# Attention into a gated feed-forward: the hidden units dealt four to a row, beta in sixteen pieces, and an earlier request for four units of q and k

## The chip, the core and the metric

The kernel runs on one core of a Trainium2 chip, written in Bass, with every instruction placed by hand or by the kernel's own planner. The core has TensorE (PE, with its weight loads shown as PEld), VectorE (DVE), ScalarE (ACT), GpSimd (POOL) and SyncE (SP). Transfers are issued by SP, ACT and POOL; those that change the type from float32 to bfloat16 on the way are all issued by POOL. The metric is the device time of one execution in microseconds (us). The kernel before took a median of 228.8 us in three runs (228.58 to 229.22).

## The reference

Attention over 4 batches, 8 heads, 768 positions and 64 dimensions. A query sees its own and the 127 positions before it, and the first four positions (the sinks). The result, 3072 tokens of 512 values, goes through a feed-forward with 2048 hidden units:

```
scores = scale * q @ k^T; keep = (pos < 4) or (0 <= i - j < 128)
a = softmax(scores where keep);  x = (a @ v) laid out as (3072, 512)
h = x @ w_in                      # (3072, 2048)
g = h * sigmoid(beta * h)         # beta has one value per hidden unit
out = g @ w_out                   # (3072, 512), float32
```

The kernel computes sigmoid by tanh: g' = h * (tanh(beta/2 * h) + 1), and halves the output.

## The kernel before

**Attention** is cut into 32 units: a unit is one pair of heads and one half (384 positions) of one batch. For units 0 to 11, q and k come in as float32 through SP (`load_qk`, line 522), are cast to bfloat16 (`cast`, line 621: k always on POOL; q on DVE for units 0 to 3, on POOL after that), transposed on PE (`transpose_first`, `transpose_in`, lines 652 and 634) and copied out of PSUM by DVE or ACT. Scores go through ACT's exponential, a mask on DVE, the product with v (`attend`, line 770), a division (`normalise`, lines 779 and 781) and a transpose into `xT`. Units 12 to 31 come in already as bfloat16 (`land_qk`, `land_v`, lines 552 and 561, issued by POOL) and are transposed by DMA.

**The feed-forward** takes the tokens in 8 tiles of 384 (T) and the hidden units in 16 blocks of 128 (m). `hidden_matmul` (line 814) makes a block's 128x384 from four matmuls, whose stationary operand is a 128x128 piece of `w_in16`. `tanh` on ACT (line 822) scales by a column of `beta_half`, `gate` on DVE (line 835) writes `g`, and `project` (line 843) multiplies with `w_out16`, 512 columns wide. In the first tile the blocks use four PSUM banks, two of which (`acc0`, `acc1`) are later the accumulators of `project`; block 12 and block 15 are their last users. While the second half of the first batch is attended (units 4 to 7), only products of the first tile can run beside it: the hidden blocks of the second tile need the outputs of units 4 to 7.

**The weights** come in through POOL: `w_in` in four chunks of four blocks (512 KB as bfloat16, 1 MB as read; line 578), `w_out` in eight chunks of two blocks (256 KB, 512 KB as read; line 583). A row of `w_out` is 2 KB; block m of it is rows 128m to 128m+127, so partition p of a chunk gets two rows that lie 256 KB apart, as two runs of 2 KB. Beta comes as 16 rows of 128 into 16 partitions (line 864, issued by ACT), and one transpose on PE (line 883) turns it into 128x16.

**The order** of each engine's instructions is fixed when the kernel is built. A planner (`Prog.order`, `round`, `landings`) takes the instructions in the order in which the program names them, with durations and a model of the transfers written in the code, and gives each engine, whenever it is free, the instruction that could start first; between equals, the one named earlier. On the chip an engine then works through its list and waits where a semaphore says so. So a change of one request or one duration may move any instruction of any engine. `after=` holds a transfer back until something has landed: the loads of units 4 to 7 wait for the second chunk of `w_in`, those of units 8 to 11 for `w_out` chunks 4, 6, 8 and 10 (named by their first block), and the v loads of the second batch for `w_out` 6, 8:

```
load_qk(y, x, [("w_in", 0, 4)])          # units 4 to 7, on SP
load_qk(n, x, [("w_out", 2 * n - 12)])   # units 8 to 11, on SP
load_v(2, c, [("w_out", 2 * c + 6)])     # on POOL
```

Between 12 and 35 us POOL's list is: the `w_in` chunks between casts, `k_sink` filled and the masks made (lines 444, 440, 492), two small loads of sink values, three loads of v for units 4 to 7 (line 542), the first `w_out` chunk, and then the casts of units 4 to 7 between the other seven `w_out` chunks.

Of the kernel before, what the change touches and what calls it, by code (L numbers as in the profile page):

```python
# [5 lines left out]
F32 = mybir.dt.float32  # L6
AF = mybir.ActivationFunctionType
ALU = mybir.AluOpType

B, H, S, D = 4, 8, 768, 64  # L10
NSINK, WINDOW = 4, 128
DM, DF, NOUT = 512, 2048, 512
NTOK = B * S
NPAIR = B * (H // 2)
SCALE = 1.0 / (D ** 0.5)
# [3 lines left out]
TT = 384  # L19
NT = NTOK // TT  # L20
NU = 4 * NT
NM = DF // 128
# [33 lines left out]
AGENDA = {}  # L56
for n in range(4, 8):
    for step, at in (("in", n - 4), ("sink", 16), ("a", 16), ("b", 16), ("av", 17), ("out", 18)):
        AGENDA.setdefault(at if step == "in" else at + 1 * (n - 4), []).append((n, step))
for n in range(8, NU):  # L60
    for at, step in STEPS.items():
        AGENDA.setdefault(FIRST[n] + at, []).append((n, step))
# [294 lines left out]
def bass_streamingllm_window__then__act_swish_beta_kernel(  # L357
# [21 lines left out]
    def sb(name, shape, dtype):  # L379
        ctx.append(nc.sbuf_tensor(name, list(shape), dtype))  # L380
        return ctx[-1].__enter__()
# [5 lines left out]
    xT = sb("xT", (128, 4, NTOK), BF16)  # L387
    w_in16 = sb("w_in16", (128, 4, DF), BF16)
    w_out16 = sb("w_out16", (128, NM, NOUT), BF16)
    beta_stage = sb("beta_stage", (16, 128), F32)  # L390
    beta_half = sb("beta_half", (128, NM), F32)
    ones = sb("ones", (128, 128), BF16)
    zeros = sb("zeros", (128, 384), BF16)
# [2 lines left out]
    ident32 = sb("ident32", (32, 32), F32)  # L396
# [30 lines left out]
    def pe(n):  # L427
        return {"busy": 2.5 + n / 2.4, "lag": 260.0}
# [4 lines left out]
    def dve(t):  # L433
        return {"busy": t, "lag": 140.0}
# [82 lines left out]
    def load_qk(n, x, after=(), queue="sp"):  # L517
        _, _, half, pb = place(n)
        name = "qk"[x]
        s = rows_of((q, k)[x], n, 1, half, 3)  # L520
        d = stage[name][pb][:, :, 3 * half:3 * half + 3, :].rearrange("p h c d -> p h (c d)")
        op(queue, lambda e: e.dma_start(d, s), w=[(name + "_stage", pb, half)], after=after,  # L522
           dma=f"{name}{pb}_{half}", seq="loads " + queue, **transfer(2 * TT * D * 4, 290 if n not in (1, 2) or x else 170, 520.0))
# [47 lines left out]
           w=[("qkT", pb, half)], dma=f"t{pb}{half}", busy=1300.0, lag=1300.0)  # L571

    w_in_src = moe_w_in.rearrange("(c p) f -> p c f", p=128)
    w_out_src = moe_w_out.rearrange("(m p) n -> p m n", p=128)

    def load_w_in(m, ms, after=()):
        here = slice(m * 128, (m + ms) * 128)
# [2 lines left out]
           dma=f"wi{m}", late=0.0 if m else 800.0, **transfer(DM * ms * 128 * 4, 385, 740.0, 3.0))  # L580

    def load_w_out(m, ms, after=()):
        op("gp", lambda e: e.dma_start(w_out16[:, m:m + ms, :], w_out_src[:, m:m + ms, :]), after=after,
           w=[("w_out", mm) for mm in range(m, m + ms)],
           dma=f"wo{m}", **transfer(ms * 128 * NOUT * 4, 416, 740.0, 3.0))

# [28 lines left out]
    def cast(n):  # L615
        _, _, half, pb = place(n)
        z = n % NQK
        here = slice(3 * half, 3 * half + 3)
        for x, name in enumerate("qk"):
            eng = "dve" if n < 4 and x == 0 else "gp"  # L620
            op(eng, lambda e, x=x, name=name, eng=eng: (e.copy if eng == "act" else e.tensor_copy)(  # L621
                qk16[z][:, x, :, :, :], stage[name][pb][:, :, here, :].rearrange("p h c d -> p c h d")),
               r=[(name + "_stage", pb, half)], w=[(name + "16", z)],
               **(dve(300.0) if eng == "dve" else {"busy": 460.0, "lag": 100.0}))
# [186 lines left out]
    def hidden_matmul(i, c):  # L811
        T, m = i // NM, i % NM
        bank, name = hidden_bank(i)
        op("pe", lambda e: e.matmul(  # L814
            bank, w_in16[:, c, m * 128:(m + 1) * 128], xT[:, c, T * TT:(T + 1) * TT],
            start=(c == 0), stop=(c == 3)),
           r=[("w_in", c, m), ("xT", T, c)], w=[name], **pe(TT))

# [22 lines left out]
    def project(T, t, m, bank, name, eng="act", cols=slice(0, NOUT), queue="sp"):  # L841
# [19 lines left out]


    constants()
    op("act", lambda e: e.dma_start(beta_stage[:, :], moe_beta.rearrange("(m p) -> m p", p=128)),
       w=["beta_stage"], dma="beta", busy=500.0, lag=100.0)
    for n in range(4):
        for x in range(2):
# [1 line left out]
    for c in range(6):  # L869
        load_v32(c // 3, c % 3)  # L870
    op("act", lambda e: e.activation(scratch[:, :], ones32[:, 0:1], AF.Exp, bias=0.0, scale=1.0),
       r=["ones32"], w=["scratch"], busy=1500.0)
    cast(0)
    cast(1)
    cast_v(0)
# [4 lines left out]

    select(ident32[:, :], ones32[:, :], [[1, 32]], ALU.is_equal, 0.0, 0, -1, ["ones32"], ["ident32"])
    transpose_first(0)
    op("pe", lambda e: nc.tensor.transpose(acc[1][:, 0:16], beta_stage[:, :], ident32[0:16, 0:16]),
       r=["beta_stage", "ident32"], w=["acc1"], **pe(64))
    op("dve", lambda e: e.tensor_scalar(beta_half[:, :], acc[1][:, 0:16], 0.5, None, ALU.mult),
       x=["acc1"], w=["beta"], **dve(100.0))

    def first_scores(n):
# [12 lines left out]
    for n in range(4):  # L901
        if n < 2:
            transpose_first(n + 2)
        if n < 3:
            first_scores(n + 1)
        if n == 2:
            for y in range(4, 8):
                for x in range(2):
                    load_qk(y, x, [("w_in", 0, 4)])
            fill("gp", k_sink[:, :, :], 0.0, ["k_sink"], busy=1800.0, after=[("v", 3, 0, 0)])  # L910
            masks([("v", 3, 0, 0)])
            load_sinks(0, [("v", 3, 0, 0)])
            for c in range(3):
                load_v(1, c, [("v", 3, 0, 0)])
            load_w_out(0, 2, [("v", 3, 0, 0)])
        bank = (acc[1], "acc1") if n < 3 else (h_ps[:, 0, :], "h0")
        attend(n, *bank)
        normalise(n, *bank)
# [122 lines left out]
```

## Time and profile before

| | |
|---|---|
| time of the profiled execution | 228.59 us |
| its span | 226.9 us |
| median of three runs | 228.8 us |
| PE busy | 220.0 us of the span |
| ACT, DVE, POOL busy | 141.3, 132.6, 125.7 us |
| hidden matmul, four of a block back to back | 0.65 us |
| granted TensorE clock | full throughout |
| read from HBM | 27.34 MB |

The span is what lies between the first and last instruction of the program; 1.7 us lie around it. A busy PE in these rows includes the tail of each matmul, which overlaps the next, so a PE that shows 2.00 of 2.00 us has no hole, and one that shows less has at least that hole. Sizes in the DMA rows of queue q0 (POOL's) are the bytes written, in bfloat16; twice as many were read. Queue q1 is SP's.

### The profile page before, as it was taken

The numbers are of one execution on the slowest core, as the hardware profiler recorded it, in microseconds if no ns is written. First come the engines' busy times: TensorE is split into PE (matmuls) and PEld (weight loads), VectorE is DVE, ScalarE is ACT, GpSimd is POOL, SyncE is SP. The second block draws the span as 40 slices with busy tenths as digits, with TensorE's granted clock in tenths as the row PEclk, the third lists the DMA queues.
The fourth block names the chain that finished last, engine by engine and source line by source line (L and its number), as shares of the span: only waits on it lengthen the run. The fifth ranks groups of instructions, "written<-read, shape, count | busy, mean of one in ns | idle before, by whom it ended". The sixth has DMA issues, their size and how long they took to land.

```text
span 226.9 us, 4463 instructions
## 1 busy us (share of the span) xinstructions
PE 220.0 (97%) x1761; PEld 122.1 (54%) x1761; DVE 132.6 (58%) x264; ACT 141.3 (62%) x224; POOL 125.7 (55%) x191
## 2 busy tenths in 40 slices
PE   7999989999999999999999999999999999999995
PEld 4665545555555555555555555555555555555454
DVE  5466777488975776566565656555656564443200
ACT  1877796197586877566657766666656755555311
POOL 4689992899994979695939396876300000000000
PEclk9999999999999999999999999999999999999999
DMA  6999999999998999999999999998921012110122
GB/s 172 251 172 179 276 194 205 257 228 139 118 138 124 124 117 151 120 167 144 116 113 135 99 138 147 96 165 119 94 80 53 20 57 64 49 46 0 58 83 92
DMA packets 96901, 28.92 MB, mean 127 GB/s; under 512 B 83424, under 2 KB 93936, under 8 KB 96880
## 3 DMA queue, kind: packets, MB, share of 16 engines
q0 software_dynamic: 59232, 10.92, 65.7%
q1 hardware_dynamic: 34304, 16.79, 34.3%
q10 hardware_dynamic: 3344, 0.93, 1.9%
q8 instruction: 14, 0.23, 0.5%
q14 instruction: 7, 0.06, 0.1%
HBM read 27.34 MB, written 6.29 MB: 148 GB/s over the span
## 4 chain that ended last, share of the span: by engine, by line
PE 73%; DMA 15%; POOL 8%; issue 2%; SPq 1%; ACT 0%; POOLq 0%; ACTq 0%
PE acc L843 32%; PE h_ps L814 29%; DMA k_stage<-in_k_dram 8%; DMA w_out<-in_moe_w_out_dram 4%; PE s_ps L727 4%; PE s_ps L770 4%; POOL qk L621 3%; DMA w_in<-in_moe_w_in_dram 2%; POOL land L552 2%; PE h_ps L843 2%; POOL v_aug L561 1%; PE s_ps L759 1%; PE s_ps L670 1%; SPq L522 1%; POOL v_aug L532 0%
## 5 line engine op out<-in xcount | busy, mean ns | idle before, releaser
L822 ACT ACTIVATE th<-h_ps,beta_half 128x384 f32<-128x384 f32 x120 | 69.4, 581 | 59.7 <-PE h_ps L814 59.1
L843 PE MATMUL acc<-w_out,g 128*128 128x512 bf16 x368 | 99.7, 380 | 0.0
L814 PE MATMUL h_ps<-xT,w_in 128*128 128x384 bf16 x480 | 96.2, 326 | 0.0
L835 DVE SCALAR_TENSOR_TENSOR g<-th,h_ps 128x384 bf16<-128x384 f32 x120 | 65.6, 550 | 44.8 <-ACT th L822 44.0
L814 PEld LDWEIGHTS h_ps<-xT,w_in 128*128 128x128 bf16 x480 | 45.6, 98 | 39.8 <-issue 0.8
L843 PEld LDWEIGHTS acc<-w_out,g 128*128 128x128 bf16 x368 | 32.8, 98 | 28.8 <-issue 3.6
L552 POOL DMA_DIRECT2D land<-in_q_dram x40 | 30.2, 760 | 24.0 <-DVE rden L779 24.0
L552 POOL DMA_DIRECT2D land<-in_k_dram x40 | 30.3, 761 | 0.0
L561 POOL DMA_DIRECT2D v_aug<-in_v_dram x40 | 30.2, 760 | 0.0
L735 ACT ACTIVATE E<-s_ps 128x1536 bf16<-128x1536 f32 x20 | 28.8, 1442 | 0.0
L741 DVE TENSOR_TENSOR E<-E,mask 128x1536 bf16<-128x1536 bf16 x20 | 19.2, 958 | 16.4 <-ACT E L735 16.4
L851 ACT ACTIVATE out_sb<-acc 128x512 f32<-128x512 f32 x23 | 13.7, 596 | 7.6 <-PE acc L843 7.4
L770 PEld LDWEIGHTS s_ps<-v_aug,E 128*128 128x128 bf16 x336 | 15.2, 97 | 3.2 <-issue 1.2
L770 PE MATMUL s_ps<-v_aug,E 128*128 128x65 bf16 x336 | 16.8, 193 | 0.0
L707 ACT ACTIVATE E<-s_ps 128x768 bf16<-128x768 f32 x17 | 13.7, 811 | 4.3 <-PE s_ps L700 4.2
L781 DVE TENSOR_TENSOR o_norm<-s_ps,rden 128x384 bf16<-128x384 f32 x28 | 15.6, 556 | 0.8
L714 DVE TENSOR_TENSOR E<-E,mask 128x768 bf16<-128x768 bf16 x16 | 9.0, 572 | 2.0 <-ACT E L707 1.3
L727 PE MATMUL s_ps<-qkT 64*128 64x256 bf16 (+2 forms) x144 | 10.1, 254 | 0.0
L759 PE MATMUL s_ps<-v_sink,E_sink 128*128 128x130 bf16 x48 | 9.3, 219 | 0.0
L621 POOL CAST qk<-k_stage 128x384 bf16<-128x384 f32 x12 | 6.5, 544 | 4.7 <-DMA k_stage<-in_k_dram 4.4
L673 ACT ACTIVATE E_sink<-s_ps 128x384 bf16<-128x384 f32 x16 | 7.8, 490 | 1.5 <-PE s_ps L670 1.5
L727 PEld LDWEIGHTS s_ps<-qkT 64*128 64x128 bf16 x144 | 4.9, 94 | 7.1 <-issue 5.8
(75 smaller groups left out, 155.2 us busy)
## 6 DMA issues: line engine op xcount, KB each, us to landing
out_dram<-out_sb SPq DMA_DIRECT2D x23, 256.0 KB, 2.7
q_stage<-in_q_dram SPq DMA_DIRECT2D x12, 192.0 KB, 7.4
k_stage<-in_k_dram SPq DMA_DIRECT2D x12, 192.0 KB, 7.9
w_in<-in_moe_w_in_dram POOLq DMA_DIRECT2D x4, 512.0 KB, 6.8
w_out<-in_moe_w_out_dram POOLq DMA_DIRECT2D x8, 256.0 KB, 9.6
land<-in_q_dram POOLq DMA_DIRECT2D x40, 48.0 KB, 3.7
land<-in_k_dram POOLq DMA_DIRECT2D x40, 48.0 KB, 4.0
v_aug<-in_v_dram POOLq DMA_DIRECT2D x40, 48.0 KB, 3.4
```

The costliest lines, as they stand in the source:

```text
L552: op("gp", lambda e, d=d, s=s: e.dma_start(d, s), w=[("land", pb, half, x, hh)], after=after, dma=f"l{pb}{half}{x}{hh}", **transfer(TT * D ...
L561: op("gp", lambda e, d=d, s=s: e.dma_start(d, s), w=[("v", pb, 3 * half + c, hh) for c in range(3)], after=after, dma=f"lv{pb}{half}{hh}", ...
L707: op("act", lambda e: e.activation(both, src[:, :, 0:TT], AF.Exp, bias=0.0, scale=SCALE), x=list(names), w=[("E", n % NE, c)], **act(768))
L727: op("pe", lambda e, at=at, w=w, kb=kb, qb=qb, nq=nq, hh=hh, rows=rows, bank=bank: e.matmul(s_ps[:, 2 * hh + bank, at:at + w], keys_of(pb, ...
L735: op("act", lambda e: e.activation(E[z][:, :, :], src, AF.Exp, bias=0.0, scale=SCALE), x=list(S_NAMES), w=[("E", z, 0), ("E", z, 1)], **ac ...
L741: op("dve", lambda e: e.tensor_tensor(E[z][:, :, :], E[z][:, :, :], m.unsqueeze(1).to_broadcast([128, 2, 768]), ALU.mult), r=[("E", z, 0), ...
L770: last=(x == len(kbs) - 1): e.matmul(av_ps[:, at + hh * D1:at + hh * D1 + D1], E[z][:, hh, col:col + 128], v_aug[:, pb, hh, kb, 0:D1], sta ...
L781: op("dve", lambda e: e.tensor_tensor(o_norm[o][:, :, :, :].rearrange("p m h d -> p (m h) d"), src[:, :, 0:D], rden[z][:, :].unsqueeze(2). ...
L814: op("pe", lambda e: e.matmul(bank, w_in16[:, c, m * 128:(m + 1) * 128], xT[:, c, T * TT:(T + 1) * TT], start=(c == 0), stop=(c == 3)), r= ...
L822: op("act", lambda e: e.activation(th[i % 3][:, :], bank, AF.Tanh, bias=0.0, scale=beta_half[:, m:m + 1]), x=[name], r=["beta"], w=[("th", ...
L835: op("dve", lambda e: e.scalar_tensor_tensor(g[T % 2][:, m, :], th[i % 3][:, :], 1.0, bank, ALU.add, ALU.mult), r=[("th", i % 3)], x=[name ...
L843: op("pe", lambda e: e.matmul(bank[:, 0:width], g[T % 2][:, m, t * 128:(t + 1) * 128], w_out16[:, m, cols], start=(m == 0), stop=(m == NM ...
```

## The change

Four things change together.

1. The hidden units are dealt to blocks in another way. Within each group of 512 units, block 4g+j now holds units 512g + 4p + j (p from 0 to 127) instead of 128 neighbours. Partition p of a `w_out` chunk then reads two rows that are neighbours, one run of 4 KB. The columns of `w_in16` that a hidden matmul loads as its stationary operand are now every fourth one: a step of 8 bytes in place of 2. How `w_in` is loaded does not change.
2. Beta follows the same deal. It is loaded as sixteen pieces of 128 values into four partitions, with four values of padding between the pieces; DVE copies it into four closed rows of 512; four transposes with a column step of four give 128x16, and the halving writes it in block order.
3. The loads of units 4 to 7 wait for the first chunk of `w_in` in place of the second.
4. On POOL the first `w_out` chunk is named before the three v loads of units 4 to 7, not behind them.

The rewritten line of `AGENDA` gives the same numbers as before.

```
+PER = 4
-    beta_stage = sb("beta_stage", (16, 128), F32)
+    beta_stage = sb("beta_stage", (NM // PER, PER, 132), F32)
+    beta_rows = sb("beta_rows", (NM // PER, 128 * PER), F32)
...
-    w_out_src = moe_w_out.rearrange("(m p) n -> p m n", p=128)
+    w_out_src = moe_w_out.rearrange("(g p j) n -> p g j n", p=128, j=PER)
...
-        op("gp", lambda e: e.dma_start(w_out16[:, m:m + ms, :], w_out_src[:, m:m + ms, :]), after=after,
+        op("gp", lambda e: e.dma_start(w_out16[:, m:m + ms, :].rearrange("p j n -> p (j n)"),
+                                         w_out_src[:, m // PER, m % PER:m % PER + ms, :].rearrange("p j n -> p (j n)")), after=after,
...
-            bank, w_in16[:, c, m * 128:(m + 1) * 128], xT[:, c, T * TT:(T + 1) * TT],
+            bank, w_in16[:, c, m // PER * 512 + m % PER:m // PER * 512 + 512:PER], xT[:, c, T * TT:(T + 1) * TT],
...
-    op("act", lambda e: e.dma_start(beta_stage[:, :], moe_beta.rearrange("(m p) -> m p", p=128)),
+    op("act", lambda e: e.dma_start(beta_stage[:, :, 0:128], moe_beta.rearrange("(g r x) -> g r x", r=PER, x=128)),
...
+    op("dve", lambda e: e.tensor_copy(beta_rows[:, :].rearrange("g (r x) -> g r x", r=PER), beta_stage[:, :, 0:128]),
+       r=["beta_stage"], w=["beta_rows"], **dve(512.0))
     cast(0)
...
-    op("pe", lambda e: nc.tensor.transpose(acc[1][:, 0:16], beta_stage[:, :], ident32[0:16, 0:16]),
-       r=["beta_stage", "ident32"], w=["acc1"], **pe(64))
-    op("dve", lambda e: e.tensor_scalar(beta_half[:, :], acc[1][:, 0:16], 0.5, None, ALU.mult),
+    with P.together("pe"):
+        for j in range(PER):
+            op("pe", lambda e, j=j: nc.tensor.transpose(
+                acc[1][:, j * (NM // PER):(j + 1) * (NM // PER)], beta_rows[:, j:128 * PER:PER],
+                ident32[0:NM // PER, 0:NM // PER]),
+               r=["beta_rows", "ident32"], w=["acc1"], **pe(64))
+    op("dve", lambda e: e.tensor_scalar(beta_half[:, :].rearrange("p (g j) -> p j g", j=PER),
+                                        acc[1][:, 0:NM].rearrange("p (j g) -> p j g", j=PER),
+                                        0.5, None, ALU.mult),
...
         if n == 2:
             for y in range(4, 8):
                 for x in range(2):
-                    load_qk(y, x, [("w_in", 0, 4)])
+                    load_qk(y, x, [("w_in", 0, 0)])
             fill("gp", k_sink[:, :, :], 0.0, ["k_sink"], busy=1800.0, after=[("v", 3, 0, 0)])
             masks([("v", 3, 0, 0)])
             load_sinks(0, [("v", 3, 0, 0)])
+            load_w_out(0, 2, [("v", 3, 0, 0)])
             for c in range(3):
                 load_v(1, c, [("v", 3, 0, 0)])
-            load_w_out(0, 2, [("v", 3, 0, 0)])
```

More of the change, by code (lines that the diff above doesn't have):

```diff
@@ L58 @@
     for step, at in (("in", n - 4), ("sink", 16), ("a", 16), ("b", 16), ("av", 17), ("out", 18)):
-        AGENDA.setdefault(at if step == "in" else at + 1 * (n - 4), []).append((n, step))
+        AGENDA.setdefault(at if step == "in" else at + n - 4, []).append((n, step))
 for n in range(8, NU):
```

## The prediction

> **What bounds the kernel now.** I read the busy times of each engine over stretches of the span first, then the chain that ended last, then the instructions around PE's holes, then the DMA queues over the stretches that the chain names.
>
> ```profile
> core 0: us, PE busy (x) PEld busy (x) DVE busy (x) ACT busy (x) POOL busy (x), PEclk, DMA share, GB/s
> ...
> 25.00:27.00 2.00, 1.59 (x14) 0.70 (x12) 1.40 (x3) 1.51 (x3) 1.88 (x4) 1.00 1.22 300
> ...
> 29.00:31.00 2.00, 1.58 (x18) 0.83 (x16) 1.15 (x3) 1.93 (x5) 1.99 (x5) 1.00 2.22 173
> 31.00:33.00 2.00, 1.56 (x19) 0.64 (x18) 1.87 (x3) 2.00 (x4) 1.93 (x4) 1.00 1.47 200
> 33.00:35.00 2.00, 1.54 (x27) 0.96 (x27) 1.68 (x5) 2.00 (x4) 1.48 (x3) 1.00 1.25 207
> ...
> 50.00:55.00 5.00, 4.82 (x34) 2.37 (x33) 4.25 (x9) 3.77 (x7) 5.00 (x8) 1.00 1.92 194
> ...
> 58.00:60.00 2.00, 1.53 (x14) 0.90 (x12) 1.96 (x5) 1.14 (x2) 2.00 (x4) 1.00 1.87 150
> ...
> 65.00:210.00 145.00, 145.00 (x1109) 78.65 (x1108) 84.12 (x160) 94.29 (x146) 72.58 (x97) 1.00 0.97 102
> ```
>
> From 65 to 210 us PE has no hole, so nothing that comes earlier there is worth anything. All that a change of transfers can win between 25 and 60 us is the holes: 0.41 + 0.42 + 0.44 + 0.46 + 0.18 + 0.47 = 2.4 us, to 226.2. In 31 to 35 us ACT is full too: the exponentials of units 4 and 5. PE has holes because hidden blocks are used up and no `w_out` has landed.
>
> ```profile
> 12.45 5.50 DMA w_in<-in_moe_w_in_dram
> 18.37 7.79 DMA k_stage<-in_k_dram
> ...
> 27.81 9.58 DMA w_out<-in_moe_w_out_dram
> 37.82 7.45 DMA k_stage<-in_k_dram
> ...
> 58.58 0.53 POOL qk L621
> ```
>
> This is the chain (start, duration): `w_in`'s second chunk lands at 17.95 and lets SP ask for units 4 to 7; `w_out` 4 lands at 37.39 and lets SP ask for units 8 to 11; their casts stand in POOL's list, which is full from 50 on, and the last one at 58.58 feeds PE.
>
> ```profile
> 25.44 0.44 PEld L814 LDWEIGHTS acc<-xT,w_in 128*128 128x128 bf16 x4 [0.50 <-DMA w_in<-in_moe_w_in_dram]
> ...
> 35.08 0.55 PEld L843 LDWEIGHTS acc<-w_out,g 128*128 128x128 bf16 x4 [0.16 <-DMA w_out<-in_moe_w_out_dram]
> ...
> 59.15 0.17 PEld L634 LDWEIGHTS s_ps<-ident,qk 128*128 128x128 bf16 x3 [0.64 <-POOL qk L621]
> ```
>
> PE's three waits that matter: block 12 for the last `w_in` chunk, the first product for the first `w_out` chunk, the last transpose of unit 11 for POOL. The first chunk of `w_out` was asked for at 24.85 and landed at 34.88, ten microseconds in a queue behind v.
>
> The last views are the DMA queues (packets, MB, share) over 18 to 21, 22 to 24, 26 to 29 and 35 to 40 us.
>
> ```profile
> q0 software_dynamic: 533, 0.53, 112.4%
> ...
> q0 software_dynamic: 248, 0.24, 72.1%
> q1 hardware_dynamic: 326, 0.24, 44.3%
> ...
> q1 hardware_dynamic: 864, 0.62, 85.2%
> q0 software_dynamic: 898, 0.08, 48.6%
> ...
> q0 software_dynamic: 1060, 1.02, 123.7%
> ```
>
> Counting q0 twice (float32 is read), the reads are 355 GB/s with `w_in` alone, 360 with q/k beside it, 260 with q/k beside the small packets of sinks and v, and 408 with `w_out` alone. And SP's requests of 17.96 got no packet before 21, while a `w_in` chunk was under way.
>
> **The change, part by part.** The sum is made against the profiled execution, 228.59 us (span 226.9 and 1.7 around it), 0.2 below the median of 228.8.
>
> *Strided weight loads.* 512 hidden matmuls now load every fourth column. Before, a load takes 98 ns and the matmuls of a block follow each other every 162 ns (0.65 us for four). A load up to 162 ns stays hidden behind the matmul before it. No row has a strided load; the nearest are the contiguous one, 98 ns, and the float32 one of beta, 175 ns (four bytes a column). Bounds: nothing, to 512 x 13 ns = 6.6 us. I take nothing, because the bytes wanted are the same and the room is 64 ns. [...]
>
> *Beta.* Added: one DVE copy of 512 columns (the cast of 384 columns takes 0.54 us, so 0.7 at most), three more transposes (the one of before: load 175 ns, matmul 282 ns; 0.5 to 0.85 us on PE), a strided halving (0.18 as before). DVE is in its fills until 4.05, when beta has long landed (2.97), so nobody waits for the transfer, also with four partitions in place of sixteen. The copy delays the cast of unit 0's q (4.15) by up to 0.7. Cover: DVE then idles 1.37 us before its copy at 6.07, and ACT takes its table until 5.97 before its own. Without that cover it would cost 0.7 + 0.6. What sets the end of this stage is unit 3, whose k lands at 11.38. I take 0; bounds 0 to +0.5.
>
> *4 KB runs.* 256 KB of `w_out` take 1.28 us (1.02 MB in 5 us). Half the packets save between nothing and the gap between the 355 and 408 GB/s already seen; I take 0.05 us of a chunk, 0.15 for the three up to `w_out` 4. POOL's issue (0.70 us with 256 runs, 0.75 with `w_in`'s 512) hardly depends on their number: 0.
>
> *Units 4 to 7 asked for earlier.* SP's eight requests (0.4 to 1.1 us each) move from 17.96 to about 14.5; nothing else is queued on SP before 37.4. Their first packet came 3.7 us after the request, behind the chunk under way; the same rule puts it at about 18 instead of 21.7. What is late next is `w_in`: for 3.7 us more its queue gets 124 packets per us (248 in 2) and not 178 (533 in 3), 200 packets less, 1.6 us at 124. That is the upper bound; 0 is the lower. In 22 to 24 some of the 16 engines had probably finished `w_in`, which lowers the 124, so I take 0.9: last chunk at 26.3 in place of 25.4. PE's wait before block 12 grows by that, but behind it PE already idled for POOL's casts of unit 4, and ACT for PE (0.36 and 0.92 us). Those casts don't move: POOL's list is full of masks, sinks and v until 25.5, whenever q and k land. Half of the 0.9 I call hidden: +0.5. In return unit 5's casts need not wait for their landing (28.46), and transposes can fill PE's wait.
>
> *`w_out` 0 before v.* On POOL one issue of 0.74 us passes three of 0.9. In the queue it now stands right behind the sinks: about 29 instead of 34.9. Both accumulators allow two products per block of it, so four matmuls of 0.216 us, 0.86 us of work, can go into the holes of 29 to 35 (1.32 us). Bounds 0 (if the planner puts them behind the attention) to -1.3; I take -0.9. The price: v stands 1.28 us further back. It landed at 32.0 to 33.6 and was first used at 33.36, so without the q/k packets gone from beside it, unit 4's product with v would wait 1.3; with them gone it is covered.
>
> *`w_out` 4 and what hangs on it.* The same bytes go ahead of it, so only efficiency counts: the 0.62 MB of q/k and 0.16 MB of v and sinks that took 3.0 us at 260 GB/s take 0.62/0.36 + 0.16/0.31 = 2.2 us when apart (310 GB/s is 29 to 31 us, v nearly alone). With the 0.15 of the longer runs: 0.95 us earlier, 36.4. Units 8 to 11, POOL's list and the cast of 58.58 come earlier by about as much. This is needed: if POOL did not move, PE would wait away at 59.15 all that it had won. Beside it, part of the hole at 33 to 35 closes (-0.3) and of that at 58 to 60 (-0.2).
>
> Sum: 0 + 0 + 0.5 - 0.9 - 0.3 - 0.2 = -0.9, so 228.6 - 0.9 = **227.7 us**.
>
> **The rivals.** *Given back* (no change, 228.6; 228.1 to 229.3). PE's work is pulled forward, but POOL and ACT, both full where it matters, do not move, or the delay of `w_in` eats it. For it: POOL shows 5.00 of 5.00 in 50 to 55 and 2.00 of 2.00 in 58 to 60, and the 0.64 wait at 59.15. Against it: POOL's list there starts from landings, which come earlier. A form of it is that the early request does nothing at all, since POOL takes the casts at 25.5 anyway.
>
> *`w_in` starved* (slower, 229.6). If q/k packets alternate with `w_in`'s at once, all 1.57 MB pass before the last chunk instead of about 0.55 MB (22 to 25.4): (1.57 - 0.55) / 0.36 = 2.8 us, landing at 28.2. Of that ACT's idle 1.28 hides some and the four products take 0.5 back: about +1.0. It decides from a landing behind 27.3. Against it: the 3.7 us without a packet. [...]
>
> *Slow strided loads* (slower, 231). If a strided load takes four times the contiguous one's pace (12 loads in 0.42 us, 35 ns each, so 140), blocks still hide it, but the first load behind a short matmul does not: 28 units with such a place each, 0.1 us, 2.9 us: 230.6 after the other terms. From 162 ns on, every hidden matmul pays; at 175 it is the 6.6 us.
>
> **How the numbers follow.** 0.3%, 0.7 us, is about what a measurement of this kernel can tell from no change: 228.1 to 229.5 is the same. Sum as above 0.46 (own range 226.4 to 228.1: from all holes closed to half the gain); given back 0.24; `w_in` starved 0.16; slow loads 0.14. So faster 0.46, same 0.24, slower 0.30. The range 226.3 to 230.4 leaves out half of the last rival and a little below.
>
> **What would show it.** Right: hidden weight loads still near 98 ns; `w_out` 0 landing before 31, with line 843 between 29 and 35 us; the last `w_in` chunk between 25.5 and 27; `w_out` 4 before 37; PE's holes in 25 to 60 near 1.5 us in place of 2.4. Wrong: a load over 160 ns, PE waiting over 1.5 us for `w_in`, v landing behind 34.5, or a wait for POOL near 59 that has grown.

## The result, and the profile after

The kernel after takes 230.53 us (median of 13 runs, 229.74 to 231.17). The ratio to the kernel before is 1.0076, with a 95% interval of 1.0057 to 1.0095. So it is slower by 1.7 us, where 0.9 us less was predicted. Its profiled execution took 230.65 us, with a span of 228.9 us (before: 226.9).

The first view is the timeline of ACT at the start (start, duration in us). This is the kernel before:

```profile
0.82 0.43 ACTq L864 DMA_DIRECT2D beta_stage<-in_moe_beta_dram  x1
1.28 3.37 ACTq L528 DMA_DIRECT2D v_stage<-in_v_dram  x6
4.68 1.28 ACT L871 ACT_TABLE_LOAD   x1 [4.68 <-issue]
...
6.08 0.45 ACT L659 COPY qkT<-s_ps 128x384 bf16<-128x384 bf16 x1
```

And this is the kernel after:

```profile
0.81 1.27 ACTq L868 DMA_DIRECT2D beta_stage<-in_moe_beta_dram  x1
2.12 5.12 ACTq L531 DMA_DIRECT2D v_stage<-in_v_dram  x6
7.26 1.28 ACT L875 ACT_TABLE_LOAD   x1 [7.26 <-issue]
...
8.66 0.45 ACT L663 COPY qkT<-s_ps 128x384 bf16<-128x384 bf16 x1
```

ACT now spends 1.27 us and not 0.43 on beta's request, and 5.12 us and not 3.37 on the six v requests behind it. Its table load and its first copy, which unit 0 needs, start 2.6 us later. Of the six v requests the first four take 0.41 to 0.53 us each, as before; the last two take 1.94 and 1.04 (the last one before: 0.65). The queues fit this. Here are the DMA queues between 2 and 4 us (packets, MB, share; q1 is SP's, q10 is ACT's), before:

```profile
q1 hardware_dynamic: 472, 0.35, 53.2%
q10 hardware_dynamic: 562, 0.14, 31.9%
```

and after:

```profile
q1 hardware_dynamic: 622, 0.45, 81.6%
q10 hardware_dynamic: 36, 0.01, 2.4%
```

In these two microseconds ACT's queue moved 562 packets before, nearly all of them v's; after, it moved 36, about beta's 8 KB alone. So nearly all of v's packets come later than 4 us: from 4 to 5 us this queue moved 323. The first v chunk lands at 7.76 us in place of 4.63, the third at 9.25 in place of 7.37. POOL's list stands on these landings, as its timeline shows in the kernel after:

```profile
9.40 0.51 POOL L535 CAST v_aug<-v_stage 128x384 bf16<-128x384 f32 x1 [1.38 <-DMA v_stage<-in_v_dram]
10.23 0.94 POOL L581 DMA_DIRECT2D w_in<-in_moe_w_in_dram  x1 [0.32 <-POOL v_aug L535]
```

The first request for `w_in` was at 8.78 us before. It is 1.45 us later now. These landings also vary by themselves: in the seven profiled executions whose beta is loaded as before, the third v lands at 7.21 to 9.34 us and `w_in` is asked for at 8.68 to 10.32. The latest of them is s_rows (an execution of 229.55 us), and the ratio of that kernel is 1.0000. With four partitions on ACT's queue (five kernels) it is 9.23 to 9.66 and 10.21 to 10.65.

PE's longest wait of the first 65 us, in the view of waits (total, times, longest), is for that copy of ACT:

```profile
PE s_ps L704 <- ACT qkT L663: 2.6, 1, 2.6
```

PE's busy time (the second number after the window) shows what this costs, in two stretches and in the one from PE's first matmul of scores to its first product with v. Before:

```profile
5.00:10.00 5.00, 4.70 (x45) 2.90 (x42) 2.04 (x4) 3.90 (x7) 2.65 (x5) 1.00 1.19 280
6.77:10.29 3.52, 3.43 (x36) 1.92 (x36) 1.33 (x3) 2.66 (x5) 2.47 (x5) 1.00 1.19 282
...
25.00:60.00 35.00, 32.62 (x306) 18.07 (x304) 26.61 (x54) 23.78 (x39) 29.23 (x45) 1.00 1.53 201
```

After:

```profile
5.00:10.00 5.00, 2.39 (x19) 1.62 (x18) 1.20 (x3) 2.13 (x4) 1.10 (x3) 1.00 1.16 291
9.17:13.74 4.57, 4.57 (x36) 2.66 (x36) 1.48 (x3) 2.66 (x5) 3.87 (x7) 1.00 0.84 153
...
25.00:60.00 35.00, 33.05 (x307) 20.00 (x310) 27.36 (x54) 26.04 (x42) 27.48 (x45) 1.00 1.45 210
```

The hole at the start grew from 0.30 to 2.61 us (+2.31), the holes from 25 to 60 us shrank from 2.38 to 1.95 (-0.43). Their sum, +1.88, is near the span's +2.04, but it is not the whole account. PE's first matmul of scores starts 2.40 us later (9.17 and not 6.77), behind ACT's copy. From there to the first product with v the same matmuls in the same order take 4.57 us and not 3.52, without a hole: PE works at a slower pace there (see the last section). From that product to the first hidden matmul it is 7.03 us in both. So of the 3.46 us by which the first tanh is late, 2.40 are the wait for ACT and 1.05 the slow stretch, and nothing is left for the later landing of v or the later request for `w_in`. Behind that PE regains 1.4 us, of which the holes in these rows show 0.43. The loss starts in the first 14 us, to which the prediction gave 0; the stretch from which it wanted its gain has even become a little denser.

Two more places of the kernel after. The chain that ended last (start, duration):

```profile
3.11 6.14 DMA v_stage<-in_v_dram
10.23 0.94 POOL w_in L581
...
17.02 12.15 DMA w_in<-in_moe_w_in_dram
```

The last `w_in` chunk now takes 12.15 us from request to landing at 29.16 (before: landing at 25.40). PE's wait for it has not grown, for PE itself is late. For the weight loads from 25 to 60 us the view of waits has

```profile
PEld acc L818 <- DMA w_in<-in_moe_w_in_dram: 0.4, 1, 0.4
```

against 0.5 us before. And the strided weight loads, in the view of groups with shapes kept apart (min/median/max in ns):

```profile
L818 PEld LDWEIGHTS h_ps<-xT,w_in x480: 110/113/133, 21.1 to 213.4; 128*128 128x128 bf16 x160
```

Before:

```profile
L814 PEld LDWEIGHTS h_ps<-xT,w_in x480: 95/98/99, 17.6 to 211.4; 128*128 128x128 bf16 x160
```

They take 113 ns where the contiguous ones took 98, and the blocks keep their pace: from block 48 of the feed-forward (93 us) to the end the kernel after is 2.03 us behind the kernel before, at every block.

### The profile page after: what moved, and what is told of

Read it like the earlier page. It is cut to its first block, busy times and chain, and to the rows that moved or that the text cites. A ratio compares the mean times of both kernels' runs of the same rounds, so it can differ in the third digit from the quotient of the medians.

```text
span 228.9 us, 4442 instructions
## 1 busy us (share of the span) xinstructions
PE 218.4 (95%) x1736; PEld 130.9 (57%) x1763; DVE 132.9 (58%) x265; ACT 141.2 (62%) x224; POOL 124.0 (54%) x191
## 4 chain that ended last, share of the span: by engine, by line
PE 79%; DMA 8%; ACT 4%; POOL 3%; DVE 3%; issue 2%; ACTq 1%; POOLq 0%
PE acc L847 34%; PE h_ps L818 31%; DMA w_in<-in_moe_w_in_dram 5%; PE s_ps L774 4%; PE s_ps L731 4%; DMA v_stage<-in_v_dram 3%; PE h_ps L847 2%; ACT E L711 1%; ACT th L826 1%; PE s_ps L763 1%; DVE g L839 1%; PE s_ps L674 1%; POOL w_in L581 1%; POOL v_aug L535 1%; DVE E L718 1%
## 5 line engine op out<-in xcount | busy, mean ns | idle before, releaser
L847 PE MATMUL acc<-w_out,g 128*128 128x512 bf16 x341 | 93.8, 379 | 1.7 <-issue 1.0
L818 PEld LDWEIGHTS h_ps<-xT,w_in 128*128 128x128 bf16 x480 | 53.0, 114 | 34.8 <-DVE g L839 1.3
L847 PEld LDWEIGHTS acc<-w_out,g 128*128 128x128 bf16 x368 | 32.7, 98 | 28.2 <-issue 4.7
L704 PE MATMUL s_ps<-qkT 64*128 64x128 bf16 (+2 forms) x52 | 5.9, 280 | 2.7 <-ACT qkT L663 2.6
```

Of the source, the lines that this page charges most:

```text
L818: op("pe", lambda e: e.matmul(bank, w_in16[:, c, m // PER * 512 + m % PER:m // PER * 512 + 512:PER], xT[:, c, T * TT:(T + 1) * TT], start= ...
L847: op("pe", lambda e: e.matmul(bank[:, 0:width], g[T % 2][:, m, t * 128:(t + 1) * 128], w_out16[:, m, cols], start=(m == 0), stop=(m == NM ...
```

## The experiments

All were timed beside the kernel before on the same chip; the ratio is to that. "First tanh" is the start of the first block's tanh in the profiled execution (before 18.65 us, after 22.11). It alone is no evidence: among the executions whose beta is loaded as before it lies between 18.62 and 20.62, for PE's pace at the start differs (see the last section). s_beta and a_betadirect were timed four times, the others 7 to 12 times.

| kernel | what it is | median us | ratio, 95% interval | first tanh |
|---|---|---|---|---|
| s_beta | before + beta alone | 231.01 | 1.0115 (1.0071 to 1.0160) | 22.00 |
| s_request | before + early request alone | 229.59 | 1.0047 (1.0015 to 1.0078) | 18.62 |
| s_stride | before + strided operand alone | 229.20 | 1.0015 (0.9976 to 1.0054) | 20.46 |
| s_stride5 | the same kernel, more runs | 228.73 | 0.9981 (0.9950 to 1.0011) | 20.20 |
| s_rows | before + 4 KB rows alone | 228.75 | 1.0000 (0.9973 to 1.0028) | 20.62 |
| s_swap | before + `w_out` 0 ahead of v alone | 228.81 | 1.0019 (0.9996 to 1.0041) | 18.66 |
| s_three | before + the last three together | 228.70 | 0.9980 (0.9951 to 1.0009) | 19.40 |
| s_betagp | s_beta, beta asked for by POOL | 229.43 | 1.0023 (0.9983 to 1.0063) | 20.44 |
| a_fourrows | after, beta in four rows, no pieces | 229.97 | 1.0072 (1.0044 to 1.0101) | 21.19 |
| a_betadirect | after, beta by SP in 16-byte pieces | 231.80 | 1.0147 (1.0110 to 1.0183) | 19.40 |
| a_direct_req | the same, with the old request | 230.21 | 1.0061 (1.0038 to 1.0084) | 20.14 |
| a_noreq | after, with the old request | 231.20 | 1.0092 (1.0066 to 1.0118) | 22.85 |
| a_noswap | after, `w_out` 0 behind v again | 230.95 | 1.0080 (1.0045 to 1.0114) | 22.67 |
| a_gp_req | after, beta by POOL, old request | 230.01 | 1.0043 (1.0015 to 1.0071) | 21.90 |
| a_gp_noswap_req | a_gp_req, `w_out` 0 behind v again | 229.66 | 1.0017 (0.9989 to 1.0046) | 20.74 |
| a_lategp3 | a_gp_req, beta asked for behind `w_in` | 229.48 | 1.0044 (1.0020 to 1.0067) | 19.52 |

### Each part alone

**Beta.** The theory after the result was that beta's request holds up ACT's list and v; the rival was that the early request starves `w_in`. In s_beta, the hidden units stay as they were, so the transposes read 128 neighbouring columns:

```
+    op("act", lambda e: e.dma_start(beta_stage[:, :, 0:128], moe_beta.rearrange("(g r x) -> g r x", r=PER, x=128)),
+    op("dve", lambda e: e.tensor_copy(beta_rows[:, :].rearrange("g (r x) -> g r x", r=PER), beta_stage[:, :, 0:128]),
...
+                acc[1][:, j * (NM // PER):(j + 1) * (NM // PER)], beta_rows[:, 128 * j:128 * j + 128],
```

> The kernel before, with beta alone changed: sixteen pieces into four padded rows, the DVE copy, four transposes (of neighbouring columns, since the units are not dealt). Theory A (the request of beta holds ACT's list: it takes 1.27 us to issue instead of 0.43, and v, POOL's casts of v and the first w_in request all follow late): the issue again takes about 1.3 us, the first v lands near 7.8 instead of 4.6, the first w_in request goes out at about 10.2 instead of 8.8, the first tanh starts 3 to 3.5 us later than 18.65, and the time is 2 to 3.5 us longer, 231 to 232. Theory B (the early request of units 4 to 7 starves w_in, beta is free): 228.8 within 0.7.

ACT's list has the same form as in the kernel after:

```profile
0.81 1.27 ACTq L867 DMA_DIRECT2D beta_stage<-in_moe_beta_dram  x1
2.12 4.82 ACTq L531 DMA_DIRECT2D v_stage<-in_v_dram  x6
```

`w_in` is first asked for at 10.53 us, the first tanh is 3.34 us late (2.11 of them by the later first scores, 1.24 in the slow stretch), and the time is 231.01 us. Beta alone is enough for the whole loss. The part that the prediction gave 0 (at most +0.5) costs about 2.5 us alone (1.6 to 3.7 by the interval).

**The early request.**

```
-                    load_qk(y, x, [("w_in", 0, 4)])
+                    load_qk(y, x, [("w_in", 0, 0)])
```

> The kernel before, with only the loads of units 4 to 7 released at the first w_in chunk. Theory A: no loss, 227.5 to 229.3. Theory B: the last w_in chunk lands 2 us or more later than 25.4 and the time is 1 to 2 us longer, 229.8 to 230.8.

The time is 229.59 us, +0.47%. The weight loads' waits from 20 to 35 us show where:

```profile
PEld acc L814 <- DMA w_in<-in_moe_w_in_dram: 3.9, 3, 1.8
```

and the queues from 21 to 25 us how (packets, MB, share):

```profile
q0 software_dynamic: 554, 0.55, 81.2%
q1 hardware_dynamic: 504, 0.37, 37.1%
```

554 packets of `w_in` against 504 of q and k: the two queues move nearly as many packets in these four microseconds. From 17 to 21 us it was already 433 against 285, where the kernel before moved `w_in` alone from 18 to 21. Before 17 us q and k get nothing: from 14.3 us, when SP asks, to 17 us `w_in`'s queue is alone,

```profile
q0 software_dynamic: 430, 0.43, 107.1%
```

and the first packet of q1 comes 2.7 us after the request. In the kernel before it comes 3.7 us after it (21.6 us), in the kernel after 2.8 (18.6). So what the prediction took over from the kernel before, a first packet some us after the request, holds here too. Then the sharing costs more than it counted: from 17 to 19 us `w_in`'s queue gets 137 packets, 68 per us and not 124, and by the landing of the last chunk q1 has moved 1.31 MB, where it had moved 0.69 MB before. The chunks land at 14.29, 20.55, 24.79 and 28.66 us.

**The strided operand**, in the same order of instructions on every engine as before:

```
-            bank, w_in16[:, c, m * 128:(m + 1) * 128], xT[:, c, T * TT:(T + 1) * TT],
+            bank, w_in16[:, c, m // PER * 512 + m % PER:m // PER * 512 + 512:PER], xT[:, c, T * TT:(T + 1) * TT],
```

> The kernel before, with only the columns of w_in that a hidden matmul loads dealt by four, order of every engine as before; it then takes hidden units that beta and w_out do not match, so the output is not the reference's. Theory A: a load takes about 114 ns instead of 98, stays hidden, and the time is 228.8 within 0.5. Rival C (slow strided loads): 229.8 or more, with holes of PE between 65 and 210 us.

> The kernel before with only the stationary operand read in steps of four columns (hidden units dealt otherwise than w_out and beta, so the result is another one); every engine's order is that of before. If the slower load (114 ns in place of 98) stays hidden: ratio 1.000 +- 0.002. If it shows where matmuls are short, 28 units by some 16 ns each and more: ratio 1.003 to 1.005.

1.0015 and, with more runs, 0.9981: both intervals hold 1. A load takes 113 ns (median) and stays behind the matmul before it, which takes 326 ns as before.

**The 4 KB rows** (the diff's two places of `w_out_src` alone, with the hidden units of `w_in` left as they were; the same order):

> The kernel before, with only the rows of w_out dealt, so that a partition reads one run of 4 KB; order of every engine as before; the hidden units keep their old places, so the output is not the reference's. Theory A (longer runs hardly matter): w_out chunks land 1.15 to 1.27 us apart where they are alone in the queue (1.24 to 1.31 before), and the time is 228.6 within 0.5. Rival: chunks land under 1.1 us apart and the time falls by 0.7 or more.

The ratio is 1.0000. The landings of the eight chunks are 0.84 to 1.79 us apart (36.52 to 45.76 us), in the kernel before 1.23 to 1.94 (34.88 to 45.07): no gain that these can show. POOL's issue of a chunk takes 0.54 us and not 0.70.

**`w_out` 0 ahead of v.**

```
+            load_w_out(0, 2, [("v", 3, 0, 0)])
             for c in range(3):
                 load_v(1, c, [("v", 3, 0, 0)])
-            load_w_out(0, 2, [("v", 3, 0, 0)])
```

> The kernel before, with only the first w_out chunk named before the three v loads of units 4 to 7. Prediction's step: the chunk lands before 32 instead of 34.9, four products fill holes of PE between 29 and 35 us, and the time falls by 0.3 to 0.9, 227.7 to 228.3. Rival: the v loads land as much later, unit 4's product with v waits for them, and the time stays at 228.6 or rises by up to 1.3.

The chunk lands at 30.54 us and not at 34.88. The profiled execution is shorter by 0.8 us, the medians are not: 1.0019, with 1 in the interval. Its products do go forward, as the timeline of the weight loads has it:

```profile
30.59 0.11 PEld L843 LDWEIGHTS acc<-w_out,g 128*128 128x128 bf16 x2 [0.89 <-DMA w_out<-in_moe_w_out_dram]
```

but they now stand in PE's list where PE has to wait 0.89 us for the chunk, and its holes from 25 to 60 us are 2.47 us against 2.38. They have moved: from 31 to 35 us they fell from 0.90 to 0.17, but from 28 to 31 they rose from 0.42 to 0.91 and from 35 to 37 from 0 to 0.82, where ACT is now full (2.00 of 2.00) and PE waits 0.8 us for it:

```profile
28.00:31.00 3.00, 2.09 (x18) 1.22 (x18) 2.00 (x4) 2.86 (x6) 3.00 (x6) 1.00 1.63 210
...
35.00:37.00 2.00, 1.18 (x12) 0.71 (x14) 1.81 (x6) 2.00 (x4) 0.00 (x0) 1.00 1.23 203
```

### Which property of beta's request it is

Beta in four rows of 512 straight into `beta_rows`, without the sixteen pieces and without DVE's copy:

```
-    op("act", lambda e: e.dma_start(beta_stage[:, :, 0:128], moe_beta.rearrange("(g r x) -> g r x", r=PER, x=128)),
+    op("act", lambda e: e.dma_start(beta_rows[:, :], moe_beta.rearrange("(g x) -> g x", x=128 * PER)),
```

> The kernel after, with beta asked for as four rows of 512 straight into the closed rows: four partitions, one piece each, no copy by DVE. Theory A1 (few partitions make the request slow to issue): the issue again takes about 1.3 us and the time stays at 230.0 to 231. Theory A2 (the sixteen pieces make it slow): the issue is back near 0.43 us, the first tanh at 18.2 to 20.5, and the time is 229 to 230, what the early request alone costs.

Beta's request takes 0.55 us, so the pieces made the request itself long. But the six v requests behind it still take 4.87 us (the last one 1.89), ACT's first copy starts at 7.69 us and not at 6.08, and the ratio stays at 1.0072. Shortening the request is not enough. Whether four partitions by themselves hold up what lies behind them, this run does not show. PE waits 1.8 us for ACT's copy and 1.5 us for `w_in`, so a part of its loss is the early request's. Its third v (9.66 us) and its request for `w_in` (10.65) are late, but those of s_rows are nearly as late. And its first v lands at 4.90 us, nearly as early as before.

Beta in sixteen pieces as in s_beta, but asked for by POOL:

```
-    op("act", lambda e: e.dma_start(beta_stage[:, :, 0:128], moe_beta.rearrange("(g r x) -> g r x", r=PER, x=128)),
+    op("gp", lambda e: e.dma_start(beta_stage[:, :, 0:128], moe_beta.rearrange("(g r x) -> g r x", r=PER, x=128)),
```

> The kernel before with beta in sixteen pieces, copied and transposed four times as in the change, but asked for by POOL and not by ACT. If what costs the 2.2 us is the request's place ahead of v on ACT's list: v's six requests take 3.4 us again and end near 4.2, ACT's table load starts near 4.2, the third v lands near 7.4, w_in is first asked for near 8.8 to 9.3, and the time is 228.8 to 229.4 us. If the small pieces themselves slow the transfers behind them, whoever asks: the third v still lands behind 9.0, w_in is asked for behind 10, and the time is 230.5 us or more. POOL's own list should not matter, it idles for 2 us before its first cast.

```profile
0.81 3.65 ACTq L531 DMA_DIRECT2D v_stage<-in_v_dram  x6
4.48 1.28 ACT L874 ACT_TABLE_LOAD   x1 [4.48 <-issue]
```

ACT's table load is back at 4.48 us, the third v lands at 7.42, `w_in` is asked for at 9.02, and the ratio falls from 1.0115 to 1.0023, whose interval holds 1. The pieces, the copy and the four transposes are all still there, so most of beta's loss is its place on ACT, ahead of v. No run separates ACT's list from ACT's queue. The expectation that POOL's list would not matter was wrong in the small: the identity and the masks that POOL makes come over 1 us later, and PE waits 1.1 us for a mask at the start.

Four partitions alone do not make the 36 packets that q10 moved from 2 to 4 us in the kernel after: in a_fourrows, also with four partitions, it moved 405 in the same two microseconds. Moving beta's request behind the v loads on ACT's own list, or to SP in the same pieces, was not tried.

Beta by SP behind q and k, in pieces of 16 bytes straight into 128 partitions, which needs neither copy nor transposes; and the same with the request for units 4 to 7 as before:

```
+    op("sp", lambda e: e.dma_start(beta_stage[:, :].rearrange("p (g j) -> p g j", j=PER),
+                                   moe_beta.rearrange("(g p j) -> p g j", p=128, j=PER)),
```

> The kernel after, with beta asked for by SP behind q and k of units 0 to 3, as 16-byte pieces straight into 128 partitions, then halved by DVE: no request on ACT, no copy, no transposes. Theory A: v lands as before, the first tanh is back at 18.2 to 19.0, and the time is 226.8 to 228.5, at or below the kernel before. Theory B: the last w_in chunk still lands behind 27.5 and the time is 229.5 to 230.8.

> The kernel after without its two suspects: beta asked for by SP behind q and k, straight into 128 partitions, and the loads of units 4 to 7 released at the second w_in chunk as before; the dealt units, the 4 KB rows and the early w_out chunk stay. Theory (beta's request and the early q and k are the whole loss): the last w_in chunk lands at 25 to 26, and the time is 227.5 to 228.8. Rival (something else in the dealt kernel costs): 229.5 or more.

In a_betadirect v and the first `w_in` request (8.60 us) are early again, and it is the slowest of all, 231.80: PE's weight loads wait 3.6 us for `w_in` (3.9 in s_request). With the old request it is 230.21. So the early request costs 1.6 us (0.9% by the two ratios) where beta does not cover it. 0.6% is left; in its profiled execution PE waits 1.6 us, once, for a `w_out` chunk.

### Do the parts add?

The kernel after with the old request, and the kernel after with `w_out` 0 behind v again:

```
-                    load_qk(y, x, [("w_in", 0, 0)])
+                    load_qk(y, x, [("w_in", 0, 4)])
```

```
-            load_w_out(0, 2, [("v", 3, 0, 0)])
             for c in range(3):
                 load_v(1, c, [("v", 3, 0, 0)])
+            load_w_out(0, 2, [("v", 3, 0, 0)])
```

> The kernel after, with only the request for units 4 to 7 moved back behind w_in's second chunk. If the two delays add, the early request's +0.8 us (as it cost alone) comes back: 229.7 us. If beta's delay covers it, because PE then waits for unit 0's attention and not for w_in, the time stays: 230.5 to 231.0 us, as beta alone gave (231.0). In both the first tanh stays near 22 us and w_in's first request near 10.2; the last w_in chunk should land near 27.5 in place of 29.2.

> The kernel after, with the first w_out chunk named behind the three v loads again. As the prediction has it, the earlier chunk is worth 0.9 us: 231.4 us, with the chunk landing at 36 to 37 us in place of 32.8 and the first product later by as much. As the swap alone showed (no difference in the medians), the time stays at 230.2 to 230.8 us wherever the chunk lands.

Neither changes the time: 1.0092 and 1.0080, with the after's 1.0076 inside both intervals. The early request, which costs +0.5% alone, costs nothing on top of beta: when PE is late by 3.5 us, chunks that are late by 3.8 us are in time. And the swap is worth nothing here either.

The kernel after with both suspects out, then also without the swap, then with beta's request by POOL moved behind `w_in`'s first one (copy, transposes and halving behind the third unit's attention):

```
-    op("act", lambda e: e.dma_start(beta_stage[:, :, 0:128], moe_beta.rearrange("(g r x) -> g r x", r=PER, x=128)),
+    op("gp", lambda e: e.dma_start(beta_stage[:, :, 0:128], moe_beta.rearrange("(g r x) -> g r x", r=PER, x=128)),
...
-                    load_qk(y, x, [("w_in", 0, 0)])
+                    load_qk(y, x, [("w_in", 0, 4)])
```

> The kernel after with both suspects taken out: beta's sixteen pieces asked for by POOL, and the request for units 4 to 7 behind w_in's second chunk. What stays are the strided stationary operand, the rows of 4 KB, and the first w_out chunk ahead of v. If beta's request and the early request are the whole loss: 228.5 to 229.2 us, no difference from before. If the kept parts pay as the prediction has it (0.9 + 0.3 + 0.2): 227.4 us. If something else of the change costs: over 229.7 us.

> The kernel after with beta's pieces asked for by POOL, the request for units 4 to 7 behind w_in's second chunk, and the first w_out chunk behind v again; strided operand, 4 KB rows and beta's copy and four transposes stay. If the chunk's place is what costs the remaining 1 us: 228.8 to 229.2 us. If it is neutral: 229.8 to 230.2 us. If it pays 0.9: 230.9 us.

```
+    op("gp", lambda e: e.dma_start(beta_stage[:, :, 0:128], moe_beta.rearrange("(g r x) -> g r x", r=PER, x=128)),
+       w=["beta_stage"], dma="beta", after=[("v", 0, 0, 0)], busy=500.0, lag=100.0)
```

> The kernel after with beta's sixteen pieces asked for by POOL behind w_in's first request (about 9.5 us), the copy, four transposes and halving behind the third unit's attention, and the request for units 4 to 7 behind w_in's second chunk. If what is left of beta's cost is its place among the first transfers, the third v lands near 7.4 again, w_in is asked for near 8.8, and the time is that of the three other parts: 228.5 to 229.0 us. If it is the copy and the transposes, or the planner's other order: 229.5 us or more.

And the three other parts together with the old beta:

```
-            bank, w_in16[:, c, m * 128:(m + 1) * 128], xT[:, c, T * TT:(T + 1) * TT],
+            bank, w_in16[:, c, m // PER * 512 + m % PER:m // PER * 512 + 512:PER], xT[:, c, T * TT:(T + 1) * TT],
...
+            load_w_out(0, 2, [("v", 3, 0, 0)])
             for c in range(3):
                 load_v(1, c, [("v", 3, 0, 0)])
-            load_w_out(0, 2, [("v", 3, 0, 0)])
```

> The kernel before with the strided stationary operand, the 4 KB rows of w_out and the first w_out chunk ahead of v, and beta as before: its columns are then not dealt like the hidden units, so the gate uses other values of beta than the reference. If these three together make the remaining 1 us: 229.6 to 230.0 us. If the remainder is beta's handling: 228.6 to 229.1 us. If the three pay as predicted: below 228.2 us.

s_three is not different from before (0.9980, 1 in the interval). So the strided operand, the 4 KB rows and the swap cost nothing together. They win at most 0.5% by the interval, and the 1.4 us (0.6%) that the prediction gave to `w_out`'s chunks lie outside it. a_gp_req and a_lategp3 should have come to 228.5 to 229.2 us if the two suspects were the whole loss. They came out at 230.01 and 229.48 (1.0043 and 1.0044), and a_gp_noswap_req at 229.66, between its expectations (1.0017, with 1 in the interval). Nearly half of the loss or more is gone, but in two of the three a rest of 0.4% stays. If the other parts cost as little here as in s_three, only beta's new handling, or the order that the planner makes with it, can hold it. It isn't the landings: in a_lategp3 the third v (7.33 us), the first `w_in` request (8.72) and its last chunk (24.80) are as early as in the kernel before, and its profiled execution took 228.66 us. But that was the fastest of its 12 executions.

The profiled executions show two places that may hold the rest, and no run tests either. In the three kernels in which POOL asks for beta first, PE waits 1.0 to 1.1 us for a mask, and the first scores start at 8.00 to 8.21 us and not at 6.77. In a_lategp3 the stretch from the first product with v to the first hidden matmul takes 7.9 us and not 7.03, with another order of PE's list and a wait of 0.5 us for a cast of POOL; a_betadirect and a_direct_req show the same 7.9, without any transpose of beta. So this rest stays open. None of the kernels beats the one before.

## Why the prediction was wrong

**Beta (predicted 0, at most +0.5; the main error).** The step said that "nobody waits for the transfer, also with four partitions in place of sixteen". It followed beta's data to their users and found slack, which was there: DVE's copy took 0.41 us, and PE waited 0.3 us for it. The cover that it named, ACT's table load until 5.97 us, was itself behind the request and now ends at 8.54. It left out what stands behind the request on its engine and on its queue. On ACT's list that is six v requests, the table load and the first copy of unit 0 (+2.6 us); on ACT's queue it is the v data, whose landing lets POOL ask for `w_in` (+1.45 us in the profiled execution, which PE does not wait for). PE's wait for ACT's copy (2.6 us) and the slow stretch behind it (1.05 us) are what the runs show in place of the 0. s_beta shows +2.5 us for this part alone, s_betagp that most of it goes when the request leaves ACT.

**Units 4 to 7 earlier (predicted +0.5, last chunk at 26.3).** Alone the part costs about 1.0 us (1.0047), and the last chunk lands at 28.66. The rule that q and k get no packet at first held: their first one came at 17.0 us, where the prediction had 18. The step that failed is the size of what follows, 3.7 us more of sharing at 124 packets per us. In s_request `w_in`'s queue got 68 per us from 17 to 19 us, and it shared with q and k until its last chunk landed. The rival "`w_in` starved" had that and the numbers right (28.2 and +1.0 us), but not its "at once": q and k got their first packet 2.7 us after the request. In the kernel after, this term is hidden behind beta's delay (a_noreq). The landing at 29.16 us there is behind 27.3, which was to decide for this rival, but PE waits just 0.2 us for it: a landing decides nothing when PE itself is late.

**`w_out` 0 before v (predicted -0.9).** The landing was predicted at 29 us: 30.54 alone, 32.79 in the kernel after. That was near, but the gain is not there: 1.0019 alone, and 1.0080 against 1.0076 without it. The assumption that failed is that four products that can start earlier close holes. In s_swap PE waits 0.89 us for the chunk in their place and 0.8 us for ACT behind them, and its holes stay at 2.47 us. Of "given back" this is half the mechanism as written: the work is pulled forward, and ACT is full where it lands. POOL did move, as the next term shows.

**`w_out` 4 earlier (predicted 36.4 us; -0.3 and -0.2).** With the swap alone it lands at 36.58, nearly as predicted. POOL's last cast for unit 11 starts at 57.62 us and not at 58.58, and the hole from 58 to 60 us shrinks from 0.47 to 0.05, as predicted or better; but the holes opened elsewhere, and the medians do not move. In the kernel after it lands at 38.60, behind `w_in`. The predicted wait for POOL near 59 us is indeed gone there: PE's stretch from 58 to 60 us has no hole left.

**4 KB rows (predicted -0.15, POOL's issue 0).** No gain is to be seen, within 0.3%. The issue did fall, from 0.70 to 0.56 us a chunk, which nobody waits for.

**Strided loads (predicted 0).** Right in the time and off in the size: 113 ns and not 98, so the bytes wanted, which are the same, do not give the whole of a load's length; it is far from the 160 that would have counted. The 175 ns of the upper bound were taken at 3 us, in the slow pace in which contiguous bf16 loads take 151 ns too.

As for the signs named ahead: `w_out` 0 before 31, the last `w_in` chunk before 27 and `w_out` 4 before 37 all failed (32.79, 29.16, 38.60), and two of the three v loads landed behind the 34.5 us that were named as wrong (34.42 to 36.20). The holes from 25 to 60 us went to 1.95, half of the way to 1.5. The time of 230.5 lies just above the range, which was built without any rival for the first 10 us. That it is near the 230.6 of "slow strided loads" is chance: the loads cost nothing.

## What to carry to other kernels

When a transfer changes its shape, price the request as well as the data: how long the issuing engine stays on it, what stands behind it on that engine's list and on that engine's queue, and what those wake up. A small load of constants belongs where nothing urgent is behind it. And delays at the start did not add here: two parts that cost 2.5 and 1.0 us alone cost 1.7 us together, so a part's worth is measured with the others in place as well as alone.

## What the runs showed of the hardware that was not expected

- An ACT request for 8 KB takes 0.43 us into sixteen partitions in rows of 512 bytes, 0.55 us into four partitions in rows of 2 KB, and 1.27 us into four partitions in sixteen pieces of 512 bytes. POOL takes 0.75 us for the sixteen pieces at the start and 0.60 us at 9.66 us (a_lategp3). The six v requests of ACT take 3.36 to 3.96 us behind the sixteen partitions or with no beta request ahead of them, and 4.75 to 5.12 behind either form with four partitions.
- A weight load of 128x128 bfloat16 with a step of 8 bytes takes 113 ns where a contiguous one takes 98.
- PE's speed in the first 15 us is not the same in each execution. Its filler matmuls (128x128) last 314 ns until 6.3 us and 219 from 7.7 us on in the profiled execution of before, but 314 until 10.4 us in s_stride5, whose order is the same. The first tanh then starts at 20.20 us in place of 18.65 (0.40 us of it by later first scores, 1.14 in the slow stretch), though the end is only 0.6 us later. In the seven executions whose beta is loaded as before, the stretch from the first scores to the first product with v takes 3.45 to 5.55 us, and in the five with four partitions on ACT 4.57 to 5.38. After a long wait the slow pace came back: in a_noreq the fillers ran at 219 ns at 5.6 us; PE then waited 2.8 us for ACT's copy, and the granted clock fell, as the stretches (PE first, the clock before the last two columns) show:

```profile
6.00:8.00 2.00, 0.30 (x6) 0.13 (x3) 1.05 (x2) 0.77 (x1) 0.42 (x1) 0.91 1.17 278
8.00:10.00 2.00, 0.86 (x5) 0.34 (x5) 0.00 (x0) 1.39 (x4) 0.59 (x2) 0.50 1.18 290
10.00:12.00 2.00, 2.00 (x16) 1.36 (x16) 0.70 (x2) 1.58 (x3) 1.72 (x3) 0.50 0.57 92
```

The fillers ran at 314 ns again until 12.4 us. What sets this pace, and why the same order starts in two ways, no run shows. In the kernel after the fillers are at 314 ns until 12.4 us too, though its row shows a granted clock of 1.00 there, with 16 matmuls in two microseconds, as at 0.50:

```profile
10.00:12.00 2.00, 2.00 (x16) 1.32 (x16) 0.67 (x2) 1.61 (x3) 1.77 (x3) 1.00 0.67 115
```

So a row of 1.00 at the start does not mean full pace, also in the kernel before, whose clock was given as full throughout: its fillers of 314 ns run at 1.00 too. How much of the 1.7 us this pace costs in the end, no run has separated.
